# A gated Fourier-mixing kernel on one Trainium2 core: tokens, W1's order in memory and the activations' sums at other places

## Chip, cores and metric

The kernel runs on one core of a Trainium2 chip. The metric is the device time of one execution in microseconds (us). Before the change it is 702.1 us, the median of three runs from 700.77 to 703.03.

## What is computed

The reference takes x (2048 tokens of 512 features), normalises each token, mixes the result by a real two-dimensional Fourier transform, and gates that with a small MLP:

```
xn = layernorm(x)
y  = Cr @ (xn @ Wd_re.T) - Ci @ (xn @ Wd_im.T)     # Real(DFT2), Cr and Ci 2048 x 2048
h  = relu(xn @ w1 + b1) ** 2                        # 512 -> 1792
g  = silu(h @ w2 + b2)                              # 1792 -> 512
out = x + y * g
```

All of it is in float32.

## The kernel before

**Number format.** A float32 operand is split into a high and a low part (`split`: ScalarE makes the high one at L69, VectorE the low one at L72), and TensorE multiplies three times (high by high, high by low, low by high: `PASSES`).

**Seven products for eight.** Every large product is made of 2 x 2 blocks with seven block products (`PRODUCTS`), which needs sums of blocks beforehand (`sums_b` at L223 to L225, `sums_a` at L229 to L231, three instructions each, on VectorE) and a `combine` behind (L262 to L265 on VectorE, and one copy by ScalarE). One unit of such work is 42 matmuls of 128x256.

**Stages.** First layernorm and the Fourier product over the tokens, in column chunks c = 0 to 7, each with eight steps j (from chunk 2 on: L322, operands made by `moving`). `stage2` (L309) multiplies a chunk by the second Fourier matrix and stores y; that of the last chunk stands behind the first unit of MLP1. The weights' blocks and sums are made beside these chunks and stored in DRAM (`w1d`, `w2d`).

MLP1 (`hidden`, L567) has 28 units: four token blocks c of 512 tokens, by seven pairs p of feature groups. A unit of even number uses the PSUM banks b2, ba and bb, one of odd number b3 and bc. ScalarE copies one quarter (L572), VectorE combines (L262 to L265), ScalarE applies relu and square (L578, L579), and h goes to DRAM (`hd`, L580). The tokens of a block come in two halves x(2c) and x(2c+1). `xt_half` loads rows with mean and scale (L334) and x transposed (L341), normalises it with two instructions (L347), makes the sums (L223 to L225), and splits tokens and sums (768 and 1024 wide) into `xT`.

MLP2 (`outer`, L610) has 28 units again: `operand` loads one h (L588), makes its sums (L229 to L231) and splits all seven blocks (1792 wide) into a buffer `ready`. The bias b2 is put into a bank ahead (L603, ScalarE), VectorE combines after each token block, and silu (L643), the product with y (L647) and the output's adding DMA (L638, POOL) follow beside the next block.

**Order.** The chunks' instructions are ordered by a scheduler. From MLP1 on each engine follows the order in which the code is written. `plan(c, p, ahead, behind)` tables what is made beside a unit, and `go` makes the next step of it: `m` rows, `x` tokens (x2 and x3 are the second block's), `w` a piece of W2 made late (`late_w2`), `l`, `s`, `f` the whole or a part of one loaded from DRAM, `h` an operand of MLP2. SP issues nearly all DMAs, in order.

**Memory.** The normalised and split x stands in eight buffers `XC`: two of their own, six in one array `block`, cut by `sixth(j, a, on)`. When chunk 7 has used one for the last time, W1's blocks p = 0 to 5 go there (`load_w1`, L502), later h's operands and W2. Such a view is shifted by `LINE` (16 columns), so it reaches into the next sixth of the array:

```
    def sixth(j, a, on=LINE):
        v = block[:, (7 - j) * 3584 + on:][:, 0:3584]
```

W1's last block (p = 6) has two buffers of its own (L507, L508). `raws` (three slots, `slot("r", n)`) and `sums` (two, `slot("t", n)`) are shared buffers, which chunks use for raw loads and sums, and MLP1 for the blocks of h.

Of the kernel before, what the change touches and what calls it, by code (L numbers as in the profile page):

```python
# [12 lines left out]
P = 128  # L13
# [8 lines left out]
LINE = 16  # L22
# [40 lines left out]
def fnet_gated_kernel(ctx, tc, x, xt, ct, wd, w1, w2, b1, b2, out):  # L63
# [28 lines left out]
    def buf(tag, shape, name, dtype=F32, bufs=1):  # L92
        return pool.tile(shape, dtype, tag=tag, bufs=bufs, name=name)
# [3 lines left out]
    def slot(tag, n):  # L97
        return shared[tag][:, 4 * n:4 * n + 4]
# [34 lines left out]

    def sixth(j, a, on=LINE):

        v = block[:, (7 - j) * 3584 + on:][:, 0:3584]
        return v.rearrange("p (a b n) -> p a b n", a=a, n=256)

    XC = [buf(f"xc{j}", [P, 7, 2, 256], f"xc{j}", F32R) if j < 2 else sixth(j, 7, 0) for j in range(NJ)]
# [368 lines left out]
            nc.sync.dma_start(b.bitcast(F32), W1D[p][:, :, 3:7])  # L508
            W1[p] = [a[:, :, n] for n in range(3)] + [b[:, :, n] for n in range(4)]

    W2_HOME = "xc0", "xc1", 5, 6, 7, "wd0", "wd1"

    FRACTION = {"l": slice(0, 3584), "s": slice(256, 3584), "f": slice(0, 256)}

    def load_w2(p, which):
        to = W2_HOME[p]
        if p not in W2:
            W2[p] = sixth(to, 2, 0) if p in (2, 3, 4) else buf(to, [P, 2, 7, 256], f"w2_{p}", F32R)
        to, src = (v.rearrange("p a b n -> p (a b n)")[:, which] for v in (W2[p], W2D[p]))
        nc.sync.dma_start(to.bitcast(F32), src)  # L520
# [27 lines left out]
    def hidden(n, c, p):  # L548
# [56 lines left out]
    def outer(m, n, g, p, cols=(0, 1)):  # L605

        a, b = H_SLOT[PRODUCTS[n][0]], B_SLOT[PRODUCTS[n][1]]
        for k in cols:
            for a_, b_ in PASSES:
                nc.tensor.matmul(m[:, k * 256:(k + 1) * 256], g[:, a_, a, k * P:(k + 1) * P], W2[p][:, b_, b],  # L610
                                 start=p == 0 and k == 0 and (a_, b_) == (HI, HI) and n not in BIASED,
                                 stop=p == NP - 1 and (a_, b_) == (LO, HI), skip_group_check=True)

# [56 lines left out]
    for c, j in steps:  # L670
# [25 lines left out]
        if c == NC - 1:  # L696

            if j == 2:
                e = buf("e", [P, 8, 256], "rows0")
                load_rows(0, e[:, 0:4])  # L700
            if j in (2, 4):
                first = xt_half(0, j // 2 - 1, lambda k: e[:, 4:8] if (j, k) == (2, "r") else
                                turn_of(k, True))
                next(first)
            if j in (3, 6):
                list(first)
                kept.clear()
# [7 lines left out]

    def tokens(c, q):

        return xt_half(c, q, lambda k: buf({"r": ("pq01", "pq11")[q], "t": "pq10"}[k], [P, 4, 256], f"x{k}{c}_{q}"))

    def go(*names):  # L720


        for v in names:
            k, n = v[0], int(v[1:])
            if k == "m":
                load_rows(n, buf("pq00", [P, 4, 256], f"rows{n}"))
            elif k in FRACTION:
                load_w2(n, FRACTION[k])
# [13 lines left out]
    for c in range(NTC - 1):  # L742
        q0, q1 = f"x{2 * c + 2}", f"x{2 * c + 3}"
        late = (c == 0) * 1
        if c:
            plan(c - 1, 4, [f"m{c + 1}", q0])
            plan(c, 0, [q1])
        else:
            plan(c, 0, [], [f"m{c + 1}", q0, q1])
        for k, p in enumerate((late, late + 1, 2)):  # L750
            plan(c, p, [], [q0])
        for p in (3, 4, 5):
            plan(c, p, [], [q1])
        if c < len(W2_LATE):
            w = f"w{W2_LATE[c]}"
            plan(c, 2, [w])
            plan(c, 6, [], [w])
            plan(c + 1, 0, [], [w])
            plan(c + 1, 1, [w])
    plan(c, 3, ["w0"])  # L760
    plan(c, 6, [], ["w0"])
    c = NTC - 1
    plan(c, 0, ["h0"], ["w0"])
    plan(c, 1, ["w1", "h1"], ["h0"])
    plan(c, 2, [], ["h0", "w1"])
    plan(c, 3, [], ["w1"])
    plan(c, 4, ["s2", "h2"], ["h1"])
    plan(c, 5, ["f2", "s3", "h4"], ["h1"])
    plan(c, 6, ["f3", "h3", "l4", "h5"], ["h2"])

    with ordered:
        before = None
        for n, (c, p) in enumerate(units):
# [168 lines left out]
```

## Time and profile before

| what | value |
|---|---|
| median of three runs | 702.1 us |
| the profiled execution | 701.72 us |
| its span in the profile | 699.9 us |
| mean granted TensorE clock | 0.998 |
| ScalarE busy | 345.9 us, 49% |
| DMA, mean | 202 GB/s |
| MLP1's first unit begins | 404.06 us |
| MLP2's first unit begins | 549.97 us |

The span is what the profile covers; 1.8 us of the execution lie around it. A row of a timeline gives its start, its duration, the engine, the source line, the operation, the tiles it writes and reads, the count of instructions taken together, and in brackets the idle time before it with what ended that. The page's busy times follow. PE is TensorE, PEld its weight loads, DVE VectorE, ACT ScalarE, POOL GpSimd; SP only issues DMAs.

### The profile page before, as it was taken

The page shows a single profiled execution, that of the slowest core. Times are in us where ns is not written, and L with a number is a line of the kernel's source. Part 1 is how long each engine was busy: PE and PEld are TensorE (multiplying, and loading weights), DVE is VectorE, ACT ScalarE, POOL GpSimd, SP SyncE. Part 2 cuts the span into 40 slices and gives each one's busy share as a digit, 9 for nine tenths or more (in the row PEclk, how much of TensorE's full clock was granted, in tenths as well). Part 3 has the DMA queues.
Part 4 walks back from the last instruction along what each step waited for, and adds up shares of the span by engine and source line. Part 5 has one row for each costly group of instructions (what it writes and reads, how often), then busy time and mean ns, then how long its engine had stood idle before and what let it go on. Part 6 is the DMA issues. An engine that isn't in the chain of part 4 may idle for free.

```text
span 699.9 us, 12729 instructions
## 1 busy us (share of the span) xinstructions
PE 683.7 (98%) x5179; PEld 646.2 (92%) x5179; DVE 577.2 (82%) x864; ACT 345.9 (49%) x461; POOL 15.0 (2%) x16
## 2 busy tenths in 40 slices
PE   8999999999999999999999999999999998999996
PEld 5778889999999999999999989999999988999995
DVE  7988975589598698797897755999999779989795
ACT  4444644334353544544452415777777844444451
POOL 0000000000000000000000000000000000202011
PEclk9999999999999999999999999999999999999999
DMA  8632450743674763835836976665737984767674
GB/s 325 231 92 92 145 168 30 244 150 123 230 252 136 272 224 121 296 127 181 295 101 251 350 311 212 210 227 212 284 123 241 362 329 151 159 177 174 164 202 90
DMA packets 52138, 141.09 MB, mean 202 GB/s; under 512 B 4928, under 2 KB 18752, under 8 KB 50752
## 3 DMA queue, kind: packets, MB, share of 16 engines
q1 hardware_dynamic: 44784, 122.46, 50.8%
q10 hardware_dynamic: 4032, 14.68, 5.2%
q0 software_dynamic: 3264, 3.15, 3.5%
q8 instruction: 40, 0.66, 0.4%
q14 instruction: 18, 0.15, 0.1%
HBM read 97.00 MB, written 46.42 MB: 205 GB/s over the span
## 4 chain that ended last, share of the span: by engine, by line
PE 84%; DVE 8%; DMA 5%; issue 1%; ACT 1%; SPq 0%; DVEq 0%; ACTq 0%
PE m_b L322 23%; PE yps L309 13%; PE m_b_o L610 7%; PE pq_b L375 7%; PE hps L567 7%; PE m_bb L322 5%; PE m_ba L322 5%; PE hps_b L567 4%; PE m L610 3%; PE hps_ba L567 2%; DMA w2raw<-in_w 2%; PE pq_ba L375 2%; PE m_bc_o L610 1%; PE pq_bc L375 1%; PE pq_bb L375 1%
## 5 line engine op out<-in xcount | busy, mean ns | idle before, releaser
L322 PE MATMUL m_b<-g,block 128*128 128x256 f32 x1080 | 129.0, 276 | 0.0
L322 PEld LDWEIGHTS m_b<-g,block 128*128 128x128 f32 x1080 | 125.5, 188 | 0.1
L69 ACT ACTIVATE g<-raws 128x768 fp32r<-128x768 f32 (+2 forms) x65 | 57.4, 885 | 88.5 <-PE m_b L322 41.1
L72 DVE TENSOR_TENSOR g<-raws,g 128x768 fp32r<-128x768 f32 (+2 forms) x65 | 65.4, 1006 | 39.3 <-ACT g L69 39.2
L309 PE MATMUL yps<-wd,pq 128*128 128x512 f32 (+1 forms) x414 | 92.8, 374 | 0.0
L309 PEld LDWEIGHTS yps<-wd,pq 128*128 128x128 f32 x414 | 74.4, 188 | 13.7
L72 DVE TENSOR_TENSOR g<-sums,g 128x1024 fp32r<-128x1024 f32 x48 | 58.6, 1221 | 12.5 <-ACT g L69 12.5
L567 PE MATMUL hps<-xT,block 128*128 128x256 f32 x504 | 59.7, 277 | 0.7 <-DVE h L265 0.5
L567 PEld LDWEIGHTS hps<-xT,block 128*128 128x128 f32 x504 | 58.2, 188 | 1.1 <-PE hps L567 0.7
L69 ACT ACTIVATE g<-sums 128x1024 fp32r<-128x1024 f32 x48 | 50.3, 1049 | 16.8 <-PE m_ba L322 7.9
L375 PE MATMUL pq_b<-g,block 128*128 128x512 f32 x180 | 47.3, 395 | 0.5 <-DVE g L72 0.4
L610 PE MATMUL m_b_o<-w,block 128*128 128x256 f32 x360 | 44.4, 279 | 2.5 <-ACT m_b_o L603 2.5
L610 PEld LDWEIGHTS m_b_o<-w,block 128*128 128x128 f32 x360 | 42.6, 188 | 3.1 <-ACT m_b_o L603 3.0
L322 PE MATMUL m_b<-g,xc 128*128 128x256 f32 x360 | 45.2, 277 | 0.0
L322 PEld LDWEIGHTS m_b<-g,xc 128*128 128x128 f32 x360 | 43.0, 188 | 0.1
L375 PEld LDWEIGHTS pq_b<-g,block 128*128 128x128 f32 x180 | 33.3, 188 | 9.5 <-DVE block L72 2.0
L223 DVE TENSOR_TENSOR sums<-raws 128x512 f32<-128x512 f32 x49 | 33.5, 684 | 1.9 <-DMA raws<-in_ct 1.7
L567 PE MATMUL hps_b<-xT,block 128*128 128x256 f32 x288 | 34.7, 276 | 0.0
L578 ACT ACTIVATE raws<-raws,b1s 128x512 f32<-128x512 f32 x42 | 28.0, 715 | 12.1 <-DVE raws L264 12.0
L69 ACT ACTIVATE block<-hr 128x1792 fp32r<-128x1792 f32 x14 | 23.9, 1704 | 20.2 <-DVE hr L231 6.2
L567 PEld LDWEIGHTS hps_b<-xT,block 128*128 128x128 f32 x288 | 33.6, 188 | 0.0
L610 PE MATMUL m_b_o<-block 128*128 128x256 f32 x270 | 32.5, 278 | 0.0
(215 smaller groups left out, 1207.6 us busy)
## 6 DMA issues: line engine op xcount, KB each, us to landing
raws<-in_ct SPq DMA_DIRECT2D x63, 512.0 KB, 3.5
w1d<-w0g SPq DMA_DIRECT2D x21, 512.0 KB, 3.3
block<-w1d SPq DMA_DIRECT2D x6, 1792.0 KB, 8.4
hd<-raws ACTq DMA_DIRECT2D x21, 512.0 KB, 4.2
hr<-hd SPq DMA_DIRECT2D x14, 512.0 KB, 4.4
y<-ysb SPq DMA_DIRECT2D x16, 256.0 KB, 3.3
fin<-y SPq DMA_DIRECT2D x16, 256.0 KB, 4.6
x<-in_x SPq DMA_DIRECT2D x7, 512.0 KB, 6.0
```

The source lines that it names most:

```text
L69: nc.scalar.activation(hi, src, AF.Copy)
L72: return nc.vector.tensor_tensor(lo, src, hi.bitcast(F32), op=ALU.subtract)
L223: nc.vector.tensor_tensor(t[:, 0:2], r[:, 0:1].to_broadcast([P, 2, 256]), r[:, 1:3], op=ALU.add)
L309: nc.tensor.matmul(ps[:, s], PQ[c, m, k // 2][:, a_, w:w + P], WD[m, k][:, b_, s], start=n == 0, stop=n > len(todo) - 3, skip_group_check= ...
L322: nc.tensor.matmul(ps[:, d * CW:(d + 1) * CW], w[:, a_, d * P:(d + 1) * P], mv(b_), start=first and d == 0 and (a_, b_) == (HI, HI), stop= ...
L375: nc.tensor.matmul(accs[c][k], w, g[:, b_, 2 * h:2 * h + 2], start=j == 0 and h == 0 and (a_, b_) == (HI, HI), stop=j == NJ - 1 and h == 1 ...
L567: nc.tensor.matmul(product(ms, k), W1[p][a][:, a_, q * P:(q + 1) * P], xT[c, q][:, b_, b], start=share not in first, stop=q == 1 and (a_, ...
L578: nc.scalar.activation(x_[:, s], x_[:, s], AF.Relu, bias=b1s[:, f:f + 1])
L610: nc.tensor.matmul(m[:, k * 256:(k + 1) * 256], g[:, a_, a, k * P:(k + 1) * P], W2[p][:, b_, b], start=p == 0 and k == 0 and (a_, b_) == ( ...
```

## The change

**W1's order in memory.** `sixth` counts the other way, so the view shifted by 16 columns reaches into the x buffer of the next step j + 1, not of j - 1. W1's block p is therefore loaded a step later of chunk 7 (`if j > 3: load_w1(j - 4)`), and blocks 4 to 6 behind MLP1's first unit.

**The second block's tokens** (x2, x3) are made around `stage2` of the last chunk, where the first unit of MLP1 has been issued. They use slots of `sums` and `raws`, "e", and "g1a" for the rows. Tokens of the third and fourth block are made one block ahead (in block 0 and 1), and w4, w5, w0 and w1 are put elsewhere in the table. W2's part 5 has a home in two pieces, so W2 has lists of slices.

**The first activations' sums.** MLP2's operands 0 to 3 are loaded and summed in MLP1; 2 and 3 stand in four "pq" buffers and are split in two pieces (1024 and 768). The operands' buffers are `sixth(5 + n % 3)` instead of `sixth(2 + n % 3)`.

**h's stores** from unit 24 on are issued by POOL, not ScalarE.

```diff
@@ sixth
-        v = block[:, (7 - j) * 3584 + on:][:, 0:3584]
+        v = block[:, (j - 2) * 3584 + on:][:, 0:3584]
@@ load_w2 (was by fractions of a piece)
-    W2_HOME = "xc0", "xc1", 5, 6, 7, "wd0", "wd1"
+    W2_HOME = "xc0", "xc1", 2, 3, 4, "wd0", "wd1"
+    SHIFTED = 5
...
+        if p == SHIFTED:
+            t = buf(to, [P, 4096], f"w2_{p}", F32R)
+            parts = (t[:, 0:3072], slice(0, 6)), (t[:, 3072 + LINE:3584 + LINE], slice(6, 7))
@@ hidden
-        nc.scalar.dma_start(HD[c, p], x_)
+        (nc.scalar if n < 24 else nc.gpsimd).dma_start(HD[c, p], x_)
@@ operand
+        if n in (2, 3):
+            e = None
+            x_, t = (buf(f"pq{a}{(a + n) % 2}", [P, 4, 256], f"h{'rt'[a]}{c}_{p}") for a in range(2))
+        else:
...
-        g = ready[c, p] = sixth(2 + n % 3, 2)
-        split(g[:, HI], g[:, LO], e[:, 0:7])
+        g = ready[c, p] = sixth(5 + n % 3, 2)
+        for s, v in ((slice(0, 4), t), (slice(4, 7), x_[:, 0:3])) if e is None else ((slice(0, 7), e[:, 0:7]),):
+            split(g[:, HI, s], g[:, LO, s], v)
@@ the last chunk
-            if j > 2:
-                load_w1(j - 3)
+            if j > 3:
+                load_w1(j - 4)
@@ tokens
+        if c == 1:
+            return xt_half(c, q, lambda k: (slot("r", 2) if k == "r" else buf("e", [P, 4, 256], f"xt{c}_{q}")) if q
+                           else slot("t", "rt".index(k)))
@@ the table, two lines of the new one
+    plan(0, 1, ["m2", "x4", "w4"])
+    plan(2, 6, ["h3"], ["h2"])
@@ MLP1
             if n == 0:
-                load_w1(5)
-                load_w1(6)
+                go("m1", "x2", "x3")
+                for v in range(4, NP):
+                    load_w1(v)
...
             if n == 0:
+                go(*["x2", "x3"] * 2)
                 stage2(NC - 1, 0)
                 stage2(NC - 1, 1, "ba")
+                go("x2", "x3")
@@ MLP2
-            go(*{0: ("l5",), 1: ("w6",)}.get(n, ()))
+            go(*["l5"] * (n == 0))
...
-            go(f"h{n + 3}")
...
-            go(f"h{n + 2}", *{2: ("w6",), 3: ("w6",)}.get(n, ()), f"h{n + 6}")
+            go(f"h{n + 2}", f"h{n + 4}", *["w6"] * (n in (0, 3)), f"h{n + 6}")
```

**How instructions move.** On VectorE behind MLP1's first unit (whose combine ends with L265), before:

```order
 L265 TENSOR_TENSOR raws<-hps_b_4155,raws 128x256
 L262 TENSOR_TENSOR raws<-hps_3_4276,raws 128x512
 L263 TENSOR_TENSOR raws<-hps_3_4276,raws 128x2x256
 L264 TENSOR_TENSOR raws<-hps_3_4276,raws 128x512
 L265 TENSOR_TENSOR raws<-hps_3_4276,raws 128x256
 L347 TENSOR_TENSOR xr_0_4215<-xr_0_4215,rows_4210 128x1024 x2
```

And now, with x2 in `sums` and x3 in `raws`:

```order
 L265 TENSOR_TENSOR raws<-hps_b_4154,raws 128x256
 L347 TENSOR_TENSOR sums<-sums,rows_4200 128x1024 x2
 L347 TENSOR_TENSOR raws<-raws,rows_4200 128x1024 x2
 L223 TENSOR_TENSOR sums<-sums 128x512
 L224 TENSOR_TENSOR sums<-sums 128x256
 L225 TENSOR_TENSOR sums<-sums 128x256
 L223 TENSOR_TENSOR xt_1_4224<-raws 128x512
...
 L72 TENSOR_TENSOR xT_0_4285<-sums,xT_0_4285 128x768
 L72 TENSOR_TENSOR xT_0_4285<-sums,xT_0_4285 128x1024
 L72 TENSOR_TENSOR xT_1_4290<-raws,xT_1_4290 128x768
 L72 TENSOR_TENSOR xT_1_4290<-xt_1_4224,xT_1_4290 128x1024
 L262 TENSOR_TENSOR raws<-hps_3_4304,raws 128x512
```

Both halves of the second block's tokens now stand ahead of the second unit's combine (hps_3), where they began behind it.

On SP in chunk 7, the difference, with - for before and + for now; w1d_903 to w1d_908 are W1's blocks 0 to 5, in_ct a raw load of the Fourier matrix, in_xt a token transfer:

```order
 L211 DMA raws<-in_ct 128x1024
 L316 DMA y_69<-ysb_3772 128x512
+L211 DMA raws<-in_ct 128x1024
 L502 DMA block<-w1d_903 128x3584
-L211 DMA raws<-in_ct 128x1024
 L316 DMA y_69<-ysb_3772 128x512
 L502 DMA block<-w1d_904 128x3584
```

```order
 L502 DMA block<-w1d_905 128x3584
 L502 DMA block<-w1d_906 128x3584
+L334 DMA rows_4200<-rows 128x256 x4
+L341 DMA sums<-in_xt 128x1024
+L341 DMA raws<-in_xt 128x1024
 L502 DMA block<-w1d_907 128x3584
 L502 DMA block<-w1d_908 128x3584
```

The last raw load goes ahead of W1's first block, and the second block's rows and tokens go ahead of W1's blocks 4 and 5.

On VectorE at the end of chunk 7, where x1's tokens (the second half of the first block) are made beside the last operands g_7_7 of chunk 7; before:

```order
 L347 TENSOR_TENSOR raws<-raws,rows_3865 128x1024 x2
 L72 TENSOR_TENSOR g_7_7_4029<-raws,g_7_7_4029 128x768
 L223 TENSOR_TENSOR sums<-raws 128x512
 L72 TENSOR_TENSOR g_7_7_4030<-sums,g_7_7_4030 128x1024
 L72 TENSOR_TENSOR xT_1_4086<-raws,xT_1_4086 128x768
```

And now:

```order
 L347 TENSOR_TENSOR raws<-raws,rows_3865 128x1024
 L72 TENSOR_TENSOR g_7_7_4028<-raws,g_7_7_4028 128x768
 L72 TENSOR_TENSOR g_7_7_4029<-sums,g_7_7_4029 128x1024
 L347 TENSOR_TENSOR raws<-raws,rows_3865 128x1024
 L223 TENSOR_TENSOR sums<-raws 128x512
 L224 TENSOR_TENSOR sums<-sums,raws 128x256
 L72 TENSOR_TENSOR xT_1_4085<-raws,xT_1_4085 128x768
```

The 1024-wide split of g_7_7 went ahead of the second L347.

On VectorE behind the last unit's combine (h_6), where MLP2 begins; before:

```order
 L72 TENSOR_TENSOR block<-hr_1_5525,block 128x1792
 L262 TENSOR_TENSOR h_6_5867<-hps_3_5823,h_6_5867 128x512
 L263 TENSOR_TENSOR h_6_5867<-hps_3_5823,h_6_5867 128x2x256
 L264 TENSOR_TENSOR h_6_5867<-hps_3_5823,h_6_5867 128x512
 L265 TENSOR_TENSOR h_6_5867<-hps_3_5823,h_6_5867 128x256
 L229 TENSOR_TENSOR hr_2_5701<-hr_2_5701 128x512
 L230 TENSOR_TENSOR hr_2_5701<-hr_2_5701 128x256
 L231 TENSOR_TENSOR hr_2_5701<-hr_2_5701 128x256
 L229 TENSOR_TENSOR raws<-raws 128x512
```

And now:

```order
 L72 TENSOR_TENSOR block<-hr_1_5244,block 128x1792
 L262 TENSOR_TENSOR h_6_5871<-hps_3_5827,h_6_5871 128x512
 L263 TENSOR_TENSOR h_6_5871<-hps_3_5827,h_6_5871 128x2x256
 L264 TENSOR_TENSOR h_6_5871<-hps_3_5827,h_6_5871 128x512
 L265 TENSOR_TENSOR h_6_5871<-hps_3_5827,h_6_5871 128x256
 L72 TENSOR_TENSOR block<-ht_2_5303,block 128x1024
 L72 TENSOR_TENSOR block<-hr_2_5302,block 128x768
 L229 TENSOR_TENSOR sums<-sums 128x512
```

The sums of the operands 2 and 3 (hr_2, and raws) are gone from there, and the splits of operand 2 follow the combine directly.

More of the change, by code (lines that the diff above doesn't have):

```diff
@@ L509, in load_w1, with load_w2 @@
             W1[p] = [a[:, :, n] for n in range(3)] + [b[:, :, n] for n in range(4)]
-    W2_HOME = "xc0", "xc1", 5, 6, 7, "wd0", "wd1"
-    FRACTION = {"l": slice(0, 3584), "s": slice(256, 3584), "f": slice(0, 256)}
-    def load_w2(p, which):
+    W2_HOME = "xc0", "xc1", 2, 3, 4, "wd0", "wd1"
+    SHIFTED = 5
+    def load_w2(p):
         to = W2_HOME[p]
[L517 to L520, printed above, removed]
+        if p == SHIFTED:
+            t = buf(to, [P, 4096], f"w2_{p}", F32R)
+            parts = (t[:, 0:3072], slice(0, 6)), (t[:, 3072 + LINE:3584 + LINE], slice(6, 7))
+        else:
+            parts = (sixth(to, 2, 0).rearrange("p a b n -> p (a b n)"), slice(0, 7)),
+        W2[p] = []
+        for t, s in parts:
+            t = t.rearrange("p (a b n) -> p a b n", a=2, n=256)
+            nc.sync.dma_start(t.bitcast(F32), W2D[p][:, :, s])
+            W2[p] += [t[:, :, n] for n in range(s.stop - s.start)]
     def late_w2(p):
@@ L529, in late_w2 @@
         if p in W2_DIRECT:
-            t = W2[p] = buf(W2_HOME[p], [P, 2, 7, 256], f"w2_{p}", F32R)
+            t = buf(W2_HOME[p], [P, 2, 7, 256], f"w2_{p}", F32R)
             split(t[:, HI], t[:, LO], e[:, 1:8])
+            W2[p] = [t[:, :, n] for n in range(7)]
             yield
@@ L579, in hidden @@
         nc.scalar.activation(x_, x_, AF.Square)
-        nc.scalar.dma_start(HD[c, p], x_)
+        (nc.scalar if n < 24 else nc.gpsimd).dma_start(HD[c, p], x_)
         yield
     def operand(n, c, p):
-        e = shared["t"] if n % 4 == 0 else shared["r"][:, 0:8] if n % 4 == 3 else \
-            buf("e" if n == 2 else "g1" + "ab"[n % 4 - 1], [P, 8, 256], f"hr{c}_{p}")
-        x_, t = e[:, 4:8], e[:, 0:4]
+        if n in (2, 3):
+            e = None
+            x_, t = (buf(f"pq{a}{(a + n) % 2}", [P, 4, 256], f"h{'rt'[a]}{c}_{p}") for a in range(2))
+        else:
+            e = shared["t"] if n % 4 == 0 else shared["r"][:, 0:8] if n % 4 == 3 else \
+                buf("g1" + "ab"[n % 4 - 1], [P, 8, 256], f"hr{c}_{p}")
+            x_, t = e[:, 4:8], e[:, 0:4]
         nc.sync.dma_start(x_, HD[c, p])
@@ L609, in outer @@
             for a_, b_ in PASSES:
-                nc.tensor.matmul(m[:, k * 256:(k + 1) * 256], g[:, a_, a, k * P:(k + 1) * P], W2[p][:, b_, b],
+                nc.tensor.matmul(m[:, k * 256:(k + 1) * 256], g[:, a_, a, k * P:(k + 1) * P], W2[p][b][:, b_],
                                  start=p == 0 and k == 0 and (a_, b_) == (HI, HI) and n not in BIASED,
@@ L716, in tokens @@
     def tokens(c, q):
-        return xt_half(c, q, lambda k: buf({"r": ("pq01", "pq11")[q], "t": "pq10"}[k], [P, 4, 256], f"x{k}{c}_{q}"))
+        if c == 1:
+            return xt_half(c, q, lambda k: (slot("r", 2) if k == "r" else buf("e", [P, 4, 256], f"xt{c}_{q}")) if q
+                           else slot("t", "rt".index(k)))
+        return xt_half(c, q, lambda k: slot("t", 0) if (k, q) == ("t", 1) else
+                       buf({"r": ("pq01", "pq11")[q], "t": "pq10"}[k], [P, 4, 256], f"x{k}{c}_{q}"))
     def go(*names):
@@ L725, in go @@
             if k == "m":
-                load_rows(n, buf("pq00", [P, 4, 256], f"rows{n}"))
-            elif k in FRACTION:
-                load_w2(n, FRACTION[k])
+                load_rows(n, buf("g1a" if n == 1 else "pq00", [P, 4, 256], f"rows{n}"))
+            elif k == "l":
+                load_w2(n)
             elif k != "h" or n < len(units):
@@ L740, in plan @@
             beside.setdefault((c, p), ([], []))[n].extend(names)
[L742 to L769, printed above, removed]
+    plan(0, 1, ["m2", "x4", "w4"])
+    plan(0, 2, ["x5"], ["x4"])
+    plan(0, 3, [], ["w4"])
+    plan(0, 4, [], ["x5"])
+    plan(0, 5, [], ["x4", "x5"])
+    plan(0, 6, [], ["w4"])
+    plan(1, 0, ["w4"], ["x4"])
+    plan(1, 1, ["m3", "x6"], ["x5"])
+    plan(1, 2, ["x7"], ["x6"])
+    plan(1, 3, [], ["x7"])
+    plan(1, 4, [], ["x6"])
+    plan(1, 5, ["w5"], ["x7"])
+    plan(1, 6, [], ["w5"])
+    plan(2, 0, [], ["x6"])
+    plan(2, 1, [], ["x7"])
+    plan(2, 2, ["h0"], ["w5"])
+    plan(2, 3, ["w5", "w0", "h1"], ["h0"])
+    plan(2, 4, ["h2"], ["w0"])
+    plan(2, 5, [], ["h1"])
+    plan(2, 6, ["h3"], ["h2"])
+    plan(3, 0, [], ["w0"])
+    plan(3, 1, ["w1", "l2"], ["h3"])
+    plan(3, 2, ["l3"], ["w1"])
+    plan(3, 3, [], ["w1"])
+    plan(3, 4, ["l4", "w6"], ["h0"])
+    plan(3, 5, ["h4"], ["h1"])
+    plan(3, 6, ["h5"])
     with ordered:
```

## Prediction

> **What bounds the kernel now.** I read the page's busy times first, then TensorE's waits, then TensorE's timeline, and last what VectorE did ahead of each wait.
>
> ```profile
> PE 683.7 (98%) x5179; PEld 646.2 (92%) x5179; DVE 577.2 (82%) x864; ACT 345.9 (49%) x461; POOL 15.0 (2%) x16
> ```
>
> TensorE (PE) is busy 98% of a span of 699.9 us and the change leaves its matmuls as they are, so the span can only shrink by the time in which TensorE stands. VectorE (DVE), 82% as a mean, is the one engine near enough to hold it up. From 420 us on (the last product of y and both MLPs) these are TensorE's waits, in us in total, times, and the longest:
>
> ```profile
> PE m_bb_o L610 <- DVE block L72: 2.8, 3, 1.5
> PE m_b_o L610 <- ACT m_b_o L603: 2.5, 3, 1.2
> PE hps L567 <- DVE h L265: 0.5, 1, 0.5
> PE hps L567 <- DVE xT L72: 0.2, 1, 0.2
> ```
>
> They sum to 6.0. The timeline of TensorE says more: the first row of a unit gives its start.
>
> ```profile
> 420.15 4.92 PE L567 MATMUL hps<-xT,block 128*128 128x256 f32 x42
> 429.67 4.92 PE L567 MATMUL hps<-xT,block 128*128 128x256 f32 x42
> ...
> 440.52 4.34 PE L567 MATMUL hps<-xT,block 128*128 128x256 f32 x36 [0.49 <-DVE h L265]
> ...
> 450.29 4.59 PE L567 MATMUL hps<-xT,block 128*128 128x256 f32 x38 [0.21 <-DVE xT L72]
> 454.72 0.84 PE L567 MATMUL hps_bb<-xT,block 128*128 128x256 f32 x6
> ...
> 549.29 0.84 PE L567 MATMUL hps<-xT,w1a 128*128 128x256 f32 x6
> 549.97 0.84 PE L610 MATMUL m_bb_o<-w,block 128*128 128x256 f32 x6
> ...
> 553.75 2.39 PE L610 MATMUL m_b_o<-w,block 128*128 128x256 f32 x18 [0.89 <-ACT m_b_o L603]
> 555.98 0.87 PE L610 MATMUL m_bb_o<-w,block 128*128 128x256 f32 x6
> ...
> 560.92 0.40 PE L610 MATMUL m_bb_o<-block 128*128 128x256 f32 x2
> 562.27 0.74 PE L610 MATMUL m_bb_o<-block 128*128 128x256 f32 x4 [0.96 <-DVE block L72]
> ...
> 578.35 0.73 PE L610 MATMUL m_bb_o<-w,block 128*128 128x256 f32 x4 [1.51 <-DVE block L72]
> ...
> 590.48 1.65 PE L610 MATMUL m_b_o<-w,block 128*128 128x256 f32 x12 [1.24 <-ACT m_b_o L603]
> ...
> 595.29 0.84 PE L610 MATMUL m_bc_o<-w,block 128*128 128x256 f32 x6
> ```
>
> Two undisturbed units take 429.67 - 420.15 = 9.52, so one takes 4.76 (42 matmuls). From 429.67 to 454.72 stand five units: 25.05 less 23.80 is **1.25 lost** in MLP1. From 549.97 to 595.29 stand eight of MLP2: 45.32 less 38.08 is **7.24 lost**. The sum, 8.49, exceeds the 6.0 of the waits because a wait costs some 0.1 beyond its own length (MLP1: 0.49 + 0.21 waited, 1.25 lost), and because the unit from 555.98 to 560.92 took 4.94 with no wait in it, 0.18 that I don't expect back. With another 0.1 for the same slow spacing about it, **8.2** hangs on waits.
>
> All these waits have one root. VectorE has almost no idle time over MLP1:
>
> ```profile
> 425.00:550.00 125.00, 124.30 (x1094) 123.93 (x1093) 117.91 (x172) 90.07 (x124) 0.00 (x0) 1.00 0.63 229
> ```
>
> The columns are the stretch, its length, then PE, PEld, DVE, ACT and POOL busy, the granted clock, and DMA: VectorE 117.91 of 125. It enters MLP2 with its operands unmade, and so TensorE outruns it there. Just before this stretch VectorE stood idle for 13.21 us:
>
> ```profile
> 425.18 0.69 DVE L262 TENSOR_TENSOR raws<-hps,raws 128x512 f32<-128x512 f32 x1 [13.21 <-PE hps L567]
> ```
>
> **Part by part: second block's tokens beside y's last products.** x2 and x3 each cost VectorE two L347, one L223, two 256-wide sums and two splits (L72). The groups from 420 us on, busy us and mean ns:
>
> ```profile
> L347 DVE TENSOR_TENSOR xr<-xr,rows 128x1024 f32<-128x1024 f32 x12 | 14.7, 1221 | 1.4 <-DMA xr<-in_xt 1.2
> ...
> L72 DVE TENSOR_TENSOR xT<-xt,xT 128x1024 fp32r<-128x1024 f32 x6 | 7.3, 1218 | 0.3 <-ACT xT L69 0.3
> ...
> L230 DVE TENSOR_TENSOR hr<-hr 128x256 f32<-128x256 f32 x14 | 6.0, 425 | 0.5
> ...
> L72 DVE TENSOR_TENSOR xT<-xr,xT 128x768 fp32r<-128x768 f32 x6 | 5.7, 947 | 0.0
> ...
> L223 DVE TENSOR_TENSOR xt<-xr 128x512 f32<-128x512 f32 x6 | 4.1, 681 | 0.0
> ```
>
> The 256-wide sums go by L230's 425. So 2.44 + 0.68 + 0.85 + 2.17 = 6.14 for one, **12.3** for both, and 13.21 of idle time to take it. The fit: unit 0's combine ends at about 412; four L347 and six sums (8 us) end near 421 even with a little slack; the splits must wait for y's products to stop reading wd0 and wd1 at 420.15, and for ScalarE's share of y's copies and four hi splits behind it, so that the last lo split ends near 426.3. Unit 1's combine (2.6, against 425.18 before) then ends at 428.9. Who waits for that is unit 3, which needs the same bank from 429.67, and in its second product only, at 430.35: 1.5 us to spare. Nothing of it lands on the path.
>
> **First activations' sums in MLP1.** h2 and h3 are loaded, added up and mostly split before MLP2. That brings 2 x 1.6 = 3.2 (sums as L223 with two L230) into MLP1. Net, VectorE's work there falls by 12.3 - 3.2 = 9.1, from 117.9 to about 109 of 125 us. The later blocks' tokens and the weights w4, w5, w0 and w1 are only redistributed; their instructions are those of before. The 1.25 of MLP1 then goes whole: the 0.49 comes from a combine that stands behind x2's work on VectorE, the 0.21 from x3's last split, both now made before.
>
> **MLP2's waits.** A lead of 9 us covers the three block waits (0.96, 1.51 and a third of 0.3): the two that I show are the longest and need VectorE 1.5 us earlier. The waits on the bias (L603) aren't alike. The late one (590.48) follows a combine of block 0 that VectorE started late:
>
> ```profile
> 588.57 1.22 DVE L262 TENSOR_TENSOR z<-m_b_o,z 128x1024 f32<-128x1024 f32 x1
> ...
> 621.38 1.22 DVE L262 TENSOR_TENSOR z<-m_b_o,z 128x1024 f32<-128x1024 f32 x1 [1.61 <-PE m_b_o L610]
> ```
>
> ```profile
> 623.85 0.84 PE L610 MATMUL m_bc_o<-w,block 128*128 128x256 f32 x6
> ```
>
> At the next block's change VectorE waited for TensorE instead, started 2.4 us ahead of the new block's first matmul (621.38 against 623.85), and no wait stands there. With the lead, block 0's combine does the same. The early one (553.75) is of the structure: TensorE goes from the last unit of MLP1 into a bank that VectorE must first empty.
>
> ```profile
> 550.41 0.68 DVE L262 TENSOR_TENSOR h<-hps,h 128x512 f32<-128x512 f32 x1
> ```
>
> Unit 27's last matmuls end at 550.13, and this combine began at 550.41, behind a split. That split stays where it is, but the three sums that stood two places ahead of it have been done earlier, so it moves up and the combine begins some 0.25 sooner, on TensorE's end. So of 0.89 + 0.1 about **0.8** stays.
>
> **W1's order in memory.** `load_w1` moves one step later, and the first W1 block now starts only when the first product of j = 3 is done, the row below: 381.1 (380.24 + 0.86) instead of 374.97. SP is in order, so it is now close ahead of x1's token transfer.
>
> ```profile
> 380.24 0.86 PE L322 MATMUL m_bb<-g,block 128*128 128x256 f32 x6
> ```
>
> ```profile
> 374.97 0.33 SPq L502 DMA_DIRECT2D block<-w1d  x1
> ...
> 385.21 0.32 SPq L502 DMA_DIRECT2D block<-w1d  x1
> 386.45 0.33 SPq L341 DMA_DIRECT2D raws<-in_xt  x1
> ```
>
> ```profile
> 375.00:380.00 5.00, 5.00 (x23) 4.13 (x22) 4.32 (x7) 2.31 (x3) 0.00 (x0) 1.00 0.83 287
> ```
>
> ```profile
> block<-w1d SPq DMA_DIRECT2D x6, 1792.0 KB, 8.4
> ```
>
> ```profile
> 394.70 2.49 DVE L347 TENSOR_TENSOR raws<-raws,rows 128x1024 f32<-128x1024 f32 x2 [2.30 <-DMA raws<-in_xt]
> ...
> 402.75 1.22 DVE L72 TENSOR_TENSOR xT<-sums,xT 128x1024 fp32r<-128x1024 f32 x1
> ```
>
> x1 was issued at 386.45 and used at 394.70, behind the W1 block of 385.21: a transfer waits for the bytes queued ahead. Now W1[0], W1[1] and x1 are 4.19 MB in a row from 381.1. At the 287 GB/s of the window in which W1[0] went nearly alone they take 14.6 us: 395.7, against 394.7. At the 8.4 us of the page's group for one block (218 GB/s) it would be 400.3; that is the far end. VectorE's order there also puts a 1024-wide split ahead of the second L347. Behind 395.7 the chain L347, two splits, L347, L223, L225, L262, split ends near 405.35, where it ended at 403.97; MLP1's unit 0 begins at 404.06 and reads this split in its second product, from about 405.2. I take **0.2** (bounds 0, and 0.15 + 400.3 - 395.7 = 4.8).
>
> Here a rule can be weighed. The Trainium skill, "DMA: Bandwidth & Descriptors", section Queues, rings and completion order, says that each DMA engine takes the descriptors of an issuer's ring in order. This trace agrees (8.2 us for x1, behind W1). If transfers shared instead, x1 would come early and this term would be 0.
>
> **The rest.** h's stores from unit 24 on go by POOL's queue: four issues, of 1.34 us each by the nearest row, on an engine that is idle there.
>
> ```profile
> 599.48 1.34 POOL L638 DMA_DIRECT2D out<-z  x1 [599.03 <-DVE z L647]
> ```
>
> I cost them at nothing (the rival below has the other end). W2's pieces and buffers, and h's turned round by three, read the same bytes; their loads are issued units ahead: nothing. For what I can't see I keep 0.3, the size of the smallest stall here (0.21 + 0.1); it could be 0 or several such.
>
> **Sum.** 8.2 - 0.8 - 0.2 - 0.3 = 6.9 less. The profiled execution took 701.72 in all (1.8 around its span) and would take 694.8. It stands 0.4 below the median of the runs, 702.1, which becomes **695.2**.
>
> **Rivals.** *x1 is late.* If the three transfers go at 218 GB/s, TensorE stands 4.8 at 405, with the tokens' split as the releaser: 695.2 + 4.6 = 699.8. For it: the W1 row's 8.4. Against: that group holds blocks that queued behind each other. 0.10.
>
> *VectorE isn't ahead.* Lead made in MLP1 is lost if its new order waits for a load (w4, w5 or an h whose buffer comes free late), as before with 3 or 4 us at a time; MLP2's block and bias waits, 8.2 - 1.25 - 0.8 = 6.1, then stay wholly or by half: 698.3 to 701.3. Against: 9 us of lead must go. 0.10.
>
> *Slow spacing.* Matmuls of the unit at 555.98 came 0.18 / 42 = 4.3 ns further apart with the granted clock at full. Should other DMA traffic bring that to 1000 more matmuls, 4.3 comes back: 699.5. Nothing shows what sets it. 0.06.
>
> *Slower: POOL's stores.* SP loads h in order, and the load of h7 into "raws" must wait until unit 25's store, now POOL's, has left that buffer; every later h load stands behind it. The load is wanted out at about 561 and the store could be done by 550: 11 us to spare. Were POOL held off while VectorE runs, by X, MLP2 stands X - 11; slower than before from X = 18, and past the 0.3% from X = 20: 705 at X = 21. Against: POOL's row took 1.34 in a stretch where VectorE was 84% busy. 0.03.
>
> ```profile
> 600.00:700.00 100.00, 93.03 (x800) 92.49 (x799) 84.41 (x105) 41.07 (x41) 14.23 (x12) 0.99 0.67 163
> ```
>
> A rule bears on that. The Trainium skill, "SBUF — State Buffer", Who interferes with whom, has GpSimd blocked while VectorE is in a two-port mode, and holds that tensor_tensor has none, so that writing descriptors isn't stopped by it. By that, X is near 0, as the row has it.
>
> *It doesn't do what it says:* tokens that land too late for the idle time leave 702. Four W1 blocks and three token transfers, 8.9 MB from 381.1, are there by 412.1 at 287 GB/s, and needed at 414. 0.02.
>
> **How the numbers follow.** Forecast 0.69 (693.3 to 697.3), x1 0.10, VectorE 0.10, spacing 0.06, POOL 0.03, no effect 0.02. What a measurement of this kernel can tell from none is 0.3%, 2.1 us: faster means below 700.0. That holds for the forecast, nearly all of x1's, half of VectorE's, and two thirds of spacing's cases: 0.87. Slower, beyond 704.2: POOL's, with 0.01 for one of two mishaps together: 0.04. The rest is 0.09. The range goes from 692.8 (all 8.49 gone, and 0.8 for what the runs differ by, 700.77 to 703.03) to 700.0 (x1's and spacing's prices, rounded up).
>
> **What would show it.** VectorE idle for under 3 us between 412 and 426, with L347 of x2 and x3 there. No wait longer than 0.1 on hps in MLP1. At MLP2's start one wait on L603 of 0.6 to 0.7, and then no wait for a block. In MLP2's first block VectorE waiting for TensorE. A wait of TensorE at 405 would speak for x1; a wait for a block behind SP's loads of h, for POOL's stores or VectorE.

## The result, and the profile after

The changed kernel takes 698.05 us (median of 14 runs, 695.99 to 701.31), the one before 701.96 beside it. The ratio is 0.9949, 95% interval 0.9933 to 0.9965, which is 3.6 us less (the medians differ by 3.9). The profiled execution took 698.08 (span 696.3); its counterpart before took 701.72, so 3.64 less where 6.9 had been forecast. The time lies inside the range (692.8 to 700.0), 2.85 above the predicted 695.2. It lies outside the 693.3 to 697.3 that the prediction gave to its own mechanism; the range reached further for x1's and the slow spacing's sake, and what took the time was neither, so that part was luck.

TensorE's waits from 400 us on, in the changed kernel (line numbers are now the changed file's: L614 is the bias, L265 ends a combine, L261 is ScalarE's copy at the start of one):

```profile
PE m_b_o L621 <- ACT m_b_o L614: 2.3, 2, 1.6
PE m_bc_o L621 <- ACT z L261: 0.3, 1, 0.3
PE hps_ba L573 <- DVE c L265: 0.3, 1, 0.3
```

The three waits for blocks, the two on hps and the late one on the bias (590.48) are gone. A wait of 1.6 on the bias at another place is new, and so are the two of 0.3. TensorE's timeline tells where each stands:

```profile
420.60 4.92 PE L573 MATMUL hps<-xT,block 128*128 128x256 f32 x42
...
549.33 0.84 PE L621 MATMUL m_bb_o<-w,block 128*128 128x256 f32 x6
...
552.93 2.32 PE L621 MATMUL m_b_o<-w,block 128*128 128x256 f32 x18 [0.72 <-ACT m_b_o L614]
...
583.69 0.84 PE L621 MATMUL m_bc_o<-w,block 128*128 128x256 f32 x6
...
613.41 0.86 PE L621 MATMUL m_bc_o<-w,block 128*128 128x256 f32 x6
...
618.68 0.97 PE L621 MATMUL m_bc_o<-w,block 128*128 128x256 f32 x6 [0.33 <-ACT z L261]
621.28 1.64 PE L621 MATMUL m_b_o<-w,block 128*128 128x256 f32 x12 [1.62 <-ACT m_b_o L614]
...
625.48 0.84 PE L621 MATMUL m_bc_o<-w,block 128*128 128x256 f32 x6
```

Where the same units begin in the kernel before, as far as the prediction doesn't show it:

```profile
588.40 0.84 PE L610 MATMUL m_bc_o<-w,block 128*128 128x256 f32 x6
...
600.05 0.84 PE L610 MATMUL m_bc_o<-block 128*128 128x256 f32 x6
...
619.09 0.84 PE L610 MATMUL m_bc_o<-w,block 128*128 128x256 f32 x6
...
628.82 0.87 PE L610 MATMUL m_bc_o<-w,block 128*128 128x256 f32 x6
```

Stage by stage:

| TensorE's first matmul of | before | after | gain so far |
|---|---|---|---|
| MLP1's second unit | 420.15 | 420.60 | -0.45 |
| MLP2 | 549.97 | 549.33 | 0.64 |
| its second block | 588.40 | 583.69 | 4.71 |
| its second block's third unit | 600.05 | 593.62 | 6.43 |
| its third block's second unit | 628.82 | 625.48 | 3.34 |
| the end of the span | 699.9 | 696.3 | 3.6 |

At 593.62 nearly all of the forecast gain was there. Three of its 6.43 us were given back by 625.48, and 2.55 of them in one place: from 613.41 to 625.48 stand two units, 12.07 where 9.52 is the undisturbed time. What TensorE waited for there is the bias. On ScalarE the bias stands behind a split and the copy that begins block 1's combine, and from the copy on ScalarE made all of it without a pause (VectorE's part of the combine began only behind the copy, too):

```profile
618.03 0.60 ACT L261 ACTIVATE z<-m_bc_o 128x512 f32<-128x512 f32 x1 [7.74 <-DMA out<-z]
618.53 1.69 ACT L69 ACTIVATE block<-raws 128x1792 fp32r<-128x1792 f32 x1
620.11 0.59 ACT L614 ACTIVATE m_ba_o<-b2s 128x512 f32<-128x512 f32 x1
620.63 0.59 ACT L614 ACTIVATE m_b_o<-b2s 128x512 f32<-128x512 f32 x1
```

The copy is to put block 1's first quarter into z, and z was still being read by block 0's output stores. These are POOL's issues, and VectorE's product ahead of the first two:

```profile
594.36 1.25 POOL L649 DMA_DIRECT2D out<-z  x1 [38.31 <-DVE z L658]
600.64 1.20 POOL L649 DMA_DIRECT2D out<-z  x1 [5.03 <-DVE block L72]
606.49 1.19 POOL L649 DMA_DIRECT2D out<-z  x1 [4.66 <-DVE hr L231]
611.71 1.18 POOL L649 DMA_DIRECT2D out<-z  x1 [4.03 <-issue]
```

```profile
593.32 1.29 DVE L658 TENSOR_TENSOR z<-z,fin 128x512 f32<-128x512 f32 x2
```

Two quarters were ready at 594.6, yet the second is issued at 600.64: the stores go one after the other, 5.2 to 6.3 us apart, and the fourth leaves z free at 618.03. In the kernel before, the same rows of ScalarE (copy and bias), the last issue and TensorE's use of the bias were

```profile
620.56 0.60 ACT L261 ACTIVATE z<-m_bc_o 128x512 f32<-128x512 f32 x1 [4.39 <-DMA out<-z]
...
623.17 0.60 ACT L603 ACTIVATE m_b_o<-b2s 128x512 f32<-128x512 f32 x1
```

```profile
614.26 1.23 POOL L638 DMA_DIRECT2D out<-z  x1 [3.70 <-issue]
```

```profile
624.53 1.52 PE L610 MATMUL m_b_o<-w,block 128*128 128x256 f32 x12
```

So ScalarE waited there too, and TensorE did not notice. Before, block 1 began at 588.40 and lost 2.13 us at once, so its last unit began at 619.09, 1.5 ahead of the copy. After, it begins at 583.69 and the last unit at 613.41, 4.6 ahead. TensorE gained 5.7 us on that place and the chain of stores only 2.5: the wait that was removed had covered it. In the kernel before, the bias behind the copy was done at 623.77 and used at 624.53, so 0.76 was to spare; 5.7 less 2.5 less 0.76 leaves 2.4 of waiting, and 2.55 were lost.

What had been forecast for VectorE stands in its rows:

```profile
412.33 2.48 DVE L347 TENSOR_TENSOR sums<-sums,rows 128x1024 f32<-128x1024 f32 x2
...
422.16 2.17 DVE L72 TENSOR_TENSOR xT<-sums,xT 128x768 fp32r<-128x768 f32 x2 [1.92 <-ACT xT L69]
...
426.26 0.69 DVE L262 TENSOR_TENSOR raws<-hps,raws 128x512 f32<-128x512 f32 x1
...
549.58 0.69 DVE L262 TENSOR_TENSOR h<-hps,h 128x512 f32<-128x512 f32 x1 [0.47 <-PE hps L573]
...
581.24 1.23 DVE L262 TENSOR_TENSOR z<-m_b_o,z 128x1024 f32<-128x1024 f32 x1 [0.61 <-PE m_b_o L621]
```

The 13.21 us of idle time are down to 1.92, and at MLP2's start and at the first block's end VectorE waits for TensorE. From 425 to 550 VectorE is busy for 111.95 us, against 117.91 before; that is 6.0 less, where 9.1 were forecast, and it was enough for the three waits.

### The profile page after: what moved, and what is told of

The parts are those of the page before. It is cut to its first block, busy times and chain, and to the rows that moved or that the text cites. A ratio compares the mean times of both kernels' runs of the same rounds, so it can differ in the third digit from the quotient of the medians.

```text
span 696.3 us, 12737 instructions
## 1 busy us (share of the span) xinstructions
PE 683.0 (98%) x5179; PEld 646.3 (93%) x5179; DVE 578.3 (83%) x866; ACT 345.4 (50%) x463; POOL 16.9 (2%) x20
## 4 chain that ended last, share of the span: by engine, by line
PE 89%; DVE 7%; issue 1%; DMA 1%; ACT 1%; POOL 0%; DVEq 0%; ACTq 0%; POOLq 0%
PE m_b L322 23%; PE yps L309 13%; PE hps L573 10%; PE pq_b L375 7%; PE m_b_o L621 7%; PE hps_b L573 5%; PE m_bb L322 5%; PE m_ba L322 5%; PE m L621 3%; PE hps_ba L573 3%; PE pq_ba L375 2%; DVE block L72 1%; PE hps_bb L573 1%; PE pq_bb L375 1%; PE m_ba_o L621 1%
## 5 line engine op out<-in xcount | busy, mean ns | idle before, releaser
L69 ACT ACTIVATE block<-hr 128x1792 fp32r<-128x1792 f32 (+1 forms) x15 | 23.8, 1587 | 21.1 <-PE m_bb_o L621 6.5
```

The lines of the kernel that those rows point to most:

```text
L69: nc.scalar.activation(hi, src, AF.Copy)
```

## The experiments

Ratios are to the kernel before, run beside each; its median moved between 700.95 and 702.24 from one set of runs to the next, so it is the ratios that can be compared across experiments, not the times. "The z wait" is the one above.

**The changed kernel again**, as the base.

> The changed kernel once more, as the base for the others. Its first profile lost 2.4 us between 617.5 and 625.5, behind ScalarE's copy L261, which waited 7.7 us for block 0's last store out<-z. Theory Z (the z buffer): that wait is there in every execution, of 1 to 3 us by the stores' own times, and makes the runs differ by more than those of before do (5.3 against 2.4 us so far). Theory S (spacing): the missing 3 us are matmuls that come further apart, so the waits in this profile are below 1 us in all after 600.

697.97 us (six runs, 697.15 to 698.56), ratio 0.9933 (0.9911 to 0.9956). The z wait is there again, 0.54 and 1.63 us long, so it belongs to the kernel. Theory S falls: there is almost no slow spacing in this execution's MLPs (from 588.68 to 612.50 five units take 23.82 where 23.80 is undisturbed), and yet the time is the same. The six runs differ by only 1.4, so what I had written of their spread isn't borne out. Where the lack of slow spacing went is told in the last section.

**z's stores begin earlier.**

```diff
                 bias(product(ms, 5), 5)
+                finish(*done, 2)
+                finish(*done, 3)
+                go(*late)
...
-            go(f"h{n + 2}", f"h{n + 4}", *["w6"] * (n in (0, 3)), f"h{n + 6}")
+            late = [f"h{n + 4}"] + ["w6"] * (n in (0, 3)) + [f"h{n + 6}"]
+            go(f"h{n + 2}", *late * (p < NP - 1 or c > 1))
...
-                for k in ((2, 3), (0,), (1,), (), (), (), ())[p] if
+                for k in ((), (0,), (1,), (), (), (), ())[p] if
```

> The changed kernel with silu, product and store of z's quarters 2 and 3 of blocks 0 and 1 moved ahead on VectorE and POOL (behind the next block's bias, ahead of two sums and a split), so the first store is issued some 5 us earlier. Theory Z: the chain of four stores ends before TensorE's last unit of block 1, the waits of 0.33 and 1.62 on L261 and L614 go, 2 to 2.4 us less than the changed kernel (ratio to before about 0.991), and the runs differ by less. Theory S: no difference over 0.5 us.

695.70 (694.06 to 697.65), ratio 0.9901 (0.9878 to 0.9925). POOL's first and last issue for block 0, and ScalarE's copy, in this kernel:

```profile
589.52 1.25 POOL L649 DMA_DIRECT2D out<-z  x1 [33.33 <-DVE z L658]
...
606.10 1.18 POOL L649 DMA_DIRECT2D out<-z  x1 [5.21 <-DVE hr L230]
```

```profile
613.46 0.60 ACT L261 ACTIVATE z<-m_bc_o 128x512 f32<-128x512 f32 x1 [3.84 <-PE m_bc_o L621]
```

The stores are no faster (up to 6.4 apart), but begin 4.8 us sooner; the copy now waits for TensorE, and both waits are gone (TensorE's two units there take 9.68, from 612.56 to 622.24). 2.3 us less by the medians and by the ratios, as theory Z has it.

**The same in the kernel before** (the same edit, with that kernel's own list of steps).

> The same edit in the kernel before. Theory Z: there block 0's stores were hidden by the 2.1 us that TensorE lost at the start of block 1, so nothing changes: ratio 0.999 to 1.001. If it is faster by over 1 us, the stores held up the kernel before as well and the wait is not new.

701.79, ratio 0.9993 (0.9977 to 1.0009): no difference. In its profile the stores begin 3 us sooner (596.53) and no engine waits for one any more. The stores weren't on the path before; the change put them there.

**h's stores all by ScalarE.**

```diff
-        (nc.scalar if n < 24 else nc.gpsimd).dma_start(HD[c, p], x_)
+        nc.scalar.dma_start(HD[c, p], x_)
```

> The changed kernel with all of h's stores issued by ScalarE as before. Theory P (POOL): h's four stores on POOL's queue make the later stores of z slower (they were 5.2 to 6.3 us apart, 4.9 before), so the spacing returns to 4.9 and some 2 us come back. Theory Z without P: the stores keep their spacing, the time is within 0.5 us of the changed kernel's.

699.16 (695.22 to 704.58), ratio 0.9963 (0.9938 to 0.9988). z's stores of block 0 are 6.1, 5.6 and 4.7 us apart, and nothing came back: theory P falls. The median is 1.2 above the changed kernel's, more than the 0.5 expected otherwise, but the runs spread over 9 us and the ratios' intervals overlap.

This execution showed two other things. The z wait stood one boundary later. Block 1's last unit began only at 615.79, late enough for block 0's stores; block 2's last unit then met block 1's, which stand 4.7 to 6.5 us apart like the others:

```profile
652.93 0.60 ACT L261 ACTIVATE z<-m_bc_o 128x512 f32<-128x512 f32 x1 [6.42 <-DMA out<-z]
```

```profile
656.48 1.65 PE L621 MATMUL m<-w,block 128*128 128x256 f32 x12 [2.09 <-ACT m L614]
```

So the chain of stores can hold up either boundary, depending on when TensorE comes to it. Earlier in the execution, x1's tokens were late:

```profile
396.87 1.23 DVE L347 TENSOR_TENSOR raws<-raws,rows 128x1024 f32<-128x1024 f32 x1 [4.33 <-DMA raws<-in_xt]
```

```profile
406.04 2.55 PE L573 MATMUL hps_b<-xT,block 128*128 128x256 f32 x20 [0.48 <-DVE xT L72]
409.70 1.68 PE L573 MATMUL hps_ba<-xT,block 128*128 128x256 f32 x12 [1.11 <-DVE c L265]
```

They were used 1.6 us later than in the first profile (395.26), and TensorE waited 1.59 instead of 0.28. The edit changes nothing at that place, so I take it for variation between executions.

**Tokens of the second block back at their old places** (in the changed kernel; the later tokens, w4 and w5 with them).

```diff
-                go("m1", "x2", "x3")
...
-                go(*["x2", "x3"] * 2)
...
-                go("x2", "x3")
...
+    plan(0, 0, [], ["m1", "x2", "x3"])
+    plan(0, 1, [], ["x2"])
+    plan(0, 2, ["w4"], ["x2"])
```

> The changed kernel with one part undone: the second block's tokens (and the later ones, w4 and w5) are made at the places of before; the operands' sums in MLP1, W1's order and h's stores stay changed. Theory L (VectorE's lead, from the 13 us that it stood idle at 412 to 425): the lead is gone and 3.2 us of sums are added to a full VectorE, so the waits on hps in MLP1 come back (1.25 us or more lost) and waits for blocks in MLP2 too: 700 to 704 us, ratio 0.998 to 1.003. Rival H (the early sums of h bring the gain): 698 to 699 as the changed kernel.

703.23 (698.24 to 706.94), ratio 1.0021 (0.9996 to 1.0045): the whole gain is lost. MLP1's waits are back, and there are more of them than before:

```profile
PE hps L573 <- DVE h L265: 1.2, 1, 1.2
PE hps L573 <- DVE xT L72: 1.1, 2, 0.8
PE hps L573 <- DVE raws L265: 0.5, 1, 0.5
```

The two of before (0.49 and 0.21) are 1.23 and 0.22 here, at the same two units; two more stand at 519.55 and 530.43 (0.83 and 0.48), where VectorE has the early sums of h beside its other work. The expected waits for blocks in MLP2 did not come; that the early sums of h see to that is likely, but not shown by this run.

**Sums of h's operands 2 and 3 back in MLP2.**

```diff
-    plan(2, 6, ["h3"], ["h2"])
-    plan(3, 1, ["w1", "l2"], ["h3"])
+    plan(2, 6, ["h3"])
+    plan(3, 1, ["w1", "l2"])
...
-            go(f"h{n + 2}", f"h{n + 4}"
+            go(*[f"h{n + 2}"] * (1 + (n < 2)), f"h{n + 4}"
```

> The changed kernel with the other part undone: the sums of operands 2 and 3 are made in MLP2 again, directly ahead of their splits (their loads stay in MLP1). Theory L: VectorE stood idle for 4 us at 552 to 556 in the changed kernel, the sums fit there, at most 0.5 us is lost at the start of MLP2: 698 to 698.5. Rival H: 1.5 to 3 us are lost there, in waits for a block: 699.5 to 701.

700.41 (698.62 to 703.48), ratio 0.9989 (0.9968 to 1.0009). One wait is new:

```profile
PE m_bb_o L621 <- DVE block L72: 0.8, 1, 0.8
```

It is for operand 3's block: 0.9 us with what goes with it, between the two expectations. The time falls where rival H has it, but of the 2.4 us to the changed kernel waits explain only 0.9. In the profiled execution another 1.3 is slow spacing (MLP1's second unit to MLP2's start took 130.00, against 128.73 in the changed kernel, with no wait in it). Whether this kernel has more of that in every run isn't shown. With either part undone, the time isn't clear of the kernel before: the two were needed together, the tokens for the lead and the sums for about 1 us at least.

**W1 another step later.**

```diff
-            if j > 3:
-                load_w1(j - 4)
+            if j > 4:
+                load_w1(j - 5)
...
-                for v in range(4, NP):
+                for v in range(3, NP):
```

> The changed kernel with W1's blocks 0 to 2 another step later in chunk 7 (three loads there, four behind MLP1's first unit), so that x1's transfer is behind two blocks instead of W1[0] and W1[1] that overlap j = 3 and 4. Theory X (x1's tokens late by W1 ahead in SP's queue): x1 lands by 1 to 3 us earlier, the wait of 0.3 to 0.5 us on hps_ba at 408 goes, MLP1's second unit begins 0.4 to 0.6 earlier (420.1). Rival: x1 is late by VectorE's order there alone, and the wait stays.

699.38 (697.5 to 702.53), ratio 0.9972 (0.9950 to 0.9994). The test missed its aim: the scheduler left W1[0] and W1[1] where they were on SP (380.81 and 385.57, x1 at 386.59) and moved later blocks only. x1 was used at 395.60 and the wait stayed (0.5).

**Both together.** The two edits above with each other.

> The earlier stores of z and the later W1 together. Theories Z and X: 694.5 to 695.5 us, 0.4 to 0.6 less than the earlier stores alone, no wait over 0.2 us of TensorE left after 400 but that on L614 at MLP2's start (0.7). If both waits were one and the same lateness moved on, the time is that of the earlier stores alone.

694.78 (694.1 to 696.01), ratio 0.9903 (0.9880 to 0.9926), the z wait gone as with the earlier stores alone, the wait at 408 still there (0.7). The median is in the expected band, but by luck: the ratio is that of the earlier stores alone (0.9901), and the wait that was to go stayed. It says no more of x1 than the run before.

**x1's transfer ahead of W1[1]**, with the earlier stores.

```diff
-        nc.sync.dma_start(r, xt[c, q])
+        xT["load"] = nc.sync.dma_start(r, xt[c, q])
...
-            if j > 3:
-                load_w1(j - 4)
+            if j == 4:
+                load_w1(0)
+            elif j > 4:
+                with tc.issue_after(xT["load"].ins):
+                    load_w1(j - 4)
```

> The earlier stores of z, and x1's transfer issued ahead of W1[1] on SP (W1[0] stays ahead of it). The run with W1 a step later had left two W1 blocks ahead of x1, so it told nothing of theory X. Theory X: x1 lands at about 391 instead of 395.3, the wait of 0.4 to 0.7 us on hps_ba goes and MLP1's second unit begins at about 420.0: 0.4 to 0.7 less than the earlier stores alone, 694 to 695 in the median. Rival: the lateness comes from VectorE's order, or the bank is late for another reason; the wait stays.

**693.35** (693.01 to 693.59), ratio 0.9893 (0.9878 to 0.9907): the fastest, 7.6 us below the kernel before (700.95 beside it). SP's issues, VectorE's first use of x1, and TensorE:

```profile
386.16 0.33 SPq L341 DMA_DIRECT2D raws<-in_xt  x1
386.59 3.64 SPq L502 DMA_DIRECT2D block<-w1d  x2
```

```profile
390.40 1.23 DVE L347 TENSOR_TENSOR raws<-raws,rows 128x1024 f32<-128x1024 f32 x1 [1.40 <-DMA raws<-in_xt]
```

```profile
419.70 1.52 PE L573 MATMUL hps<-xT,block 128*128 128x256 f32 x12
```

Issued at the same time, x1 is there 5 us earlier with one W1 block ahead of it instead of two; the wait on hps_ba is gone and MLP1's second unit begins at 419.70, against 420.49 with the earlier stores alone. Theory X holds: what makes x1 late is the queue. (The scheduler also put the second L347 ahead of the 1024-wide split again, so a small part can be VectorE's order; that can't move the landing.) The profiled execution gains 0.87 over that of the earlier stores (693.19 against 694.06). The medians differ by 2.35, but the kernel before differed by 1.3 between the two sets; by the ratios it is 0.6, and the intervals overlap, so the rows show this gain and the times alone would not.

**One z for three blocks**, stored in the order 0, 1, 2, 3, so that each quarter waits for its own store.

```diff
-                e = buf("e", [P, 4, 512], f"z{c}")
+                e = done[1] if c else buf("e", [P, 4, 512], f"z{c}")
...
-                for k in ((2, 3), (0,), (1,), (), (), (), ())[p] if
+                for k in ((0, 1), (2,), (3,), (), (), (), ())[p] if
```

> The changed kernel with one buffer z that blocks 0 to 2 share as the same tile, so that each quarter waits for its own store only and not for all four, and the quarters stored in the order 0, 1, 2, 3; POOL's issue and VectorE's work keep their places. Theory Z: ScalarE's copy at 618 waits for the first store only and stands no more than 1 us; VectorE's first combine waits for the third store (about 612), its second for the fourth (618): of the 2.3 us lost there at most 0.6 stay, 696 to 696.5 us. If something else than the buffer held the copy, nothing changes.

695.51 (694.88 to 697.64), ratio 0.9931 (0.9907 to 0.9955). POOL's issues stand where they stood (594.49 to 610.98), ScalarE's copy waits for TensorE, and of the z wait this is left:

```profile
620.75 2.33 PE L621 MATMUL m_b_o<-w,block 128*128 128x256 f32 x18 [0.55 <-ACT m_b_o L614]
```

With the stores unmoved and only the buffer's release made finer, the wait shrinks to 0.55, and the two units from 612.55 to 622.91 take 10.36 instead of 12.07. A second cure by another means, with the same answer: z was what held the copy. The rows show it, not the time: the ratio isn't clear of the changed kernel's (0.9933 and 0.9949).

## Why the prediction was right, and where it fell short

**The direction and the mechanism were right.** VectorE's 13 us of idle time took the second block's tokens: the last split ended at 426.34 (426.3 forecast) and unit 1's combine at 428.85 (428.9), and from 420 on no wait was left in MLP1. The experiment with the tokens put back lost the whole gain and brought MLP1's waits back, so the change can't do without this part; the early sums add to it.

**MLP2's first block went as forecast.** The waits for blocks are gone, the combine at 588.57 became one that waits for TensorE (581.24), and the wait at MLP2's start stayed: 0.72 long, and 549.33 to 555.09 for the first unit, 1.0 lost where I had kept 0.8. That comes from a size that the prediction had wrong: it added 0.1 to each wait, but its own row of MLP1 (0.70 waited in two stops, 1.25 lost) gives 0.28 for each, and so do MLP2's start (0.72 and 1.0) and the z wait (1.95 in two, 2.55). By 0.28 the term is 0.92.

**The step that failed** inside a range that held is the one on MLP2's late wait: "started 2.4 us ahead of the new block's first matmul (621.38 against 623.85), and no wait stands there. With the lead, block 0's combine does the same." I read that boundary (block 1 to 2) as free because TensorE had no wait there, and used it as the pattern for the boundary ahead. Free it was only as long as TensorE came late. ScalarE's row for the copy, with 4.39 us of waiting for DMA out<-z, was in the trace of before. It shows a chain (product, four stores in a row, buffer free) that ended 1.5 us behind the start of the block's last unit, and TensorE was forecast to come 6 us sooner. The term missing from the sum is 2.55 by the units' starts; the earlier stores gave back 2.3.

**x1's tokens were of the right kind and too small.** I took 0.2; the second unit began 0.45 later than before. The landing was well placed (395.7 forecast, 395.26 measured), and the need was earlier than I had it: TensorE waited for the bank that chunk 7's combine, behind x1's work on VectorE, releases (hps_ba), not for the split of the tokens. In the run with h's stores on ScalarE it waited for both, which makes the rival's mechanism (TensorE waits as long as x1 is late) a real one, at 1.6 us of its 4.8. That the landing came so close is partly luck: the 4.19 MB took 14.5 us from W1[0]'s issue at 380.73, 289 GB/s where 287 was taken from one window of before.

**The other rivals.** VectorE far enough ahead: yes. POOL's stores of h: the four issues took 0.53 to 0.71 us each. They landed later behind the issue than ScalarE's (9.1 and 7.3 us by the page's groups, against 4.9 and 3.1), but no engine waited for a load of h. Slow spacing came and went from run to run of the same kernel, so nothing here makes it a price of the change.

**The account.** 6.9 forecast and 3.64 measured on the profiled executions leave 3.26: 2.55 for z, 0.25 for x1, 0.2 at MLP2's start. The last 0.26 is a balance of small things: slow spacing took 0.75 of the four units from 593.62 to 613.41 (19.79 where 19.04 is undisturbed), and against it stand the 0.3 kept for what I couldn't see and what the profile of before lost to the same spacing behind 619.09.

## What to carry to other kernels

Before a wait is taken out, look one stage on for each chain that is not on the path only because of it: a row of an idle engine that waits for a DMA (here ScalarE for out<-z) warns that the path may come only a little earlier before the chain shows: count what is left from the end of the chain to its use (0.76 here). In this kernel a buffer that is allocated anew waits for every reader of the old one; keep the same tile, or start the stores sooner. In an in-order DMA queue, put the small transfer that is needed first ahead of the big ones that are not.

## What the hardware showed

**Accumulating stores on POOL's queue went one at a time.** Four 256 KB stores of one block never overlapped in any profile: issues stood 4.4 to 7.3 us apart, whether the data were ready or not, a transfer took 4.0 to 7.0 us from issue to landing, and each of the later ones was issued 0.3 us after the one before had landed. The plain stores of h on the same queue did overlap (issued at 540.24 and 544.99, 9.1 us to landing). The kernel's own code asks for no such wait; whether its framework or the queue makes it isn't shown.

**A short wait can cost twice.** In the second profile of the changed kernel the granted clock fell behind the z wait; the columns are as in the window rows of the prediction, with the clock third from the end, for this kernel's first profile and then its second:

```profile
620.00:624.00 4.00, 2.72 (x23) 2.72 (x24) 3.86 (x4) 2.66 (x5) 0.00 (x0) 1.00 0.04 13
```

```profile
620.00:624.00 4.00, 3.43 (x17) 3.43 (x18) 3.86 (x4) 2.66 (x5) 0.00 (x0) 0.57 0.00 0
```

```profile
617.98 0.97 PE L621 MATMUL m_bc_o<-w,block 128*128 128x256 f32 x6 [0.54 <-ACT z L261]
620.57 2.93 PE L621 MATMUL m_b_o<-w,block 128*128 128x256 f32 x12 [1.63 <-ACT m_b_o L614]
```

Twelve matmuls took 2.73 (620.57 to 623.30) instead of 1.36 (550.01 to 551.37 in the first profile): 1.4 us on top of the wait. The profile with W1 a step later shows it too (0.60 from 620 to 624); the other three profiles with this pair of waits don't. The changed kernel's second execution had hardly any slow spacing, and for this reason was no faster for it. In the six kernels with the z wait, at one boundary or the other, 26 of 62 runs had a mean granted clock of 0.995 or less; in the four without it or with 0.55 of it, none of 20 had; of the kernel before beside the experiments, 4 of 59. The Trainium skill, "TensorE: Matmul & The Clock Gate", section "HAM oscillation — how this bites in real kernels", has the clock halved by gaps longer than about 3.4 us. The halving agrees; the gap does not: here two waits of 0.54 and 1.63 with six matmuls between them were enough in some executions. The counts say that this goes with the waits; what decides in which execution isn't shown.

**Slow spacing.** Matmuls came about 4% further apart for tens of microseconds with the granted clock at 1.00, at other places in each execution: this unit of the changed kernel took 4.95 instead of 4.76 with no wait in it.

```profile
588.67 0.87 PE L621 MATMUL m_bc_o<-w,block 128*128 128x256 f32 x6
...
593.62 0.87 PE L621 MATMUL m_bc_o<-block 128*128 128x256 f32 x6
```

In the first profile of the changed kernel it took 0.94 us of the five units from 588.67 to 613.41, in the second 0.02 of the same five. I found no cause for it; that stays open.
